# Batch 0's values loaded in packed rows and put in token order by selecting products, in an attention and mixer kernel

## The chip, the cores and the metric

One core of a Trainium2 chip runs the whole program. The metric is the device time of one execution in microseconds; three runs of the kernel before are given, with their median.

## The reference

Attention over 8 batches, 8 heads, 576 tokens of 64 values, with 16 extra ("beacon") keys and values ahead of each head's own, and after it a mixer: a low-rank product over the tokens and a two-layer product over the channels.

```python
k_all = np.concatenate([beacon_k, k], axis=2)
v_all = np.concatenate([beacon_v, v], axis=2)
scores = scale * np.matmul(q, k_all.transpose(0, 1, 3, 2))
scores = np.where(causal, -1000000000.0, scores)
a = np.exp(scores - scores.max(-1, keepdims=True))
a /= a.sum(-1, keepdims=True) + 1e-09
attn = np.matmul(a, v_all)                       # 8 x 8 x 576 x 64

x = attn.transpose(0, 2, 1, 3).reshape(8, 576, 512)
h = x.transpose(0, 2, 1) @ U @ V                 # U 576 x 32, V 32 x 576
u = x + h.transpose(0, 2, 1)
out = u + np.maximum(u @ w_ch1, 0.0) @ w_ch2     # 512 -> 2048 -> 512
```

Inputs and outputs are float32. The kernel works in float16 with float32 sums.

## The kernel before, in words

The attention goes by pairs of heads: 8 batches of 4 pairs are pairs 0 to 31, so pairs 0 to 3 are batch 0 and pairs 4 to 7 batch 1. The mixer's channel products go by 9 blocks of 512 tokens. Five engines work side by side: PE (matmul), DVE and ACT (elementwise, ACT alone does exponentials), POOL (here mainly the queue that issues casting loads) and SP (the queue of transposing transfers and of stores, and of batch 0's Q and K). Each engine runs its instructions in order. The order is written out by hand in a string, `SCRIPT`, of 961 steps; each step emits its instructions on the engines at that place. The names of the steps:

- `G`, `H`, `T`: for one pair, `Gq`/`Gk` regroups the main rows of Q or K into token order (and for batch 0 casts the head rows too, unless an `H` step does that), `H` casts the head rows, `T` turns them with five PE transposes into `tps` and copies the result to `qT` or `kT`. The letter behind says which engine copies (V DVE, A ACT, G POOL), the number which pair: `TkA7` is K of pair 7, copied by ACT.
- `Sa` to `Sd`: the scores of a pair in four groups of 496, 464, 496 and 208 columns for each of its two heads, on 64 partitions each (`sps`, L316), and ACT's exponentials into `expt` (L321). `Sa0:3` puts three filler matmuls ahead. There are four `expt` tiles, so a pair waits for the products of the pair two before it.
- `M`: DVE masks the exponentials of one head (L304, L306). `A`: PE's 15 products of the exponentials with V (`po`, L331), and DVE's division into `xb` (L339, L340).
- `I1`: one filler matmul of 512 columns into `idle` (L241).
- `X`: the low-rank part of one batch (`qtp`, `ups`, into `uT`). `g`, `U`, `p`, `P`, `F`: a block's first product (`gps`, L529, four matmuls a step, evacuated by ACT as `gT`, and DVE), transposes, sums and second products.
- `k`, `q`, `v`, `b`, `w`: loads on POOL's queue of K, Q, V, the beacon keys and weights (`w12` is quarter 2 of the first weights, which `g` steps 8 to 11 read), whole (all heads) or as half `A` or `B`. `u`, `s`, `c`, `e`: the loads and casts of the mixer's small matrices. `B` fills the mask.

Batch 0 loads Q and K through SP and ACT's queue into `stm` and `sth` in float32, pair by pair. Its V is loaded by `v0A` and `v0B`, the beacon rows and five tiles of tokens for each half of the heads:

```python
beacon_load(nc.gpsimd, bsrc, dst[:, 0, :, :], hs)
for j in range(NT):
    a = Nb if j == 0 else 0
    nc.gpsimd.dma_start(
        out=dst[a : a + nq[j], j, :, :], in_=src[hs, ds(q0[j], nq[j]), :].rearrange("h p d -> p h d")
    )
```

`nq` is 112, 128, 128, 128, 80. A partition of `vs` holds one token of each head (64 values, and a column of ones) for each of the five tiles. All PSUM tiles come from one pool of 8 banks. The pool `stage` (`st0`, `st1`) has two buffers for each name, and `loads` (`hd0`, `hd1`) too; a load into a new one waits until the old one's readers are through.

Of the kernel before, what the change touches and what calls it, by code (L numbers as in the profile page):

```python
# [27 lines left out]
def kernel(  # L28
# [82 lines left out]
    ident = const.tile([P, P], F16, name="ident", tag="ident")  # L111
# [80 lines left out]
    def beacon_load(eng, src, dst, hs):  # L192
        eng.dma_start(out=dst[0:Nb], in_=src[hs].rearrange("h p d -> p h d"))
# [4 lines left out]
    def v_loads(src, bsrc, vs, hs):  # L198
        dst = vs[:, :].rearrange("p (c h e) -> p c h e", h=H, e=E)[:, :, hs, 0:D]
# [589 lines left out]
    def step(t):  # L789
        name, arg = t[0], t[1:]  # L790
        if t == "guard":
            guard()
        elif t == "sum":
            guard_sum()
        elif name == "I":
            keep_warm(pst([P, 512], F32, name="idle"), int(arg))
        elif name in "kqbv":
            b, hs = int(arg[0]), HALVES[arg[1:]]
            if name == "k":
                k_loads(b, L_of(b), hs)  # L800
# [54 lines left out]
        Sd0 Sb0 Sa0:3 I1 GqV1 TqV1 GkV2 Sc0 I1 GqV2 v0B I1 I1 Sc1 Sb1 I1 M0.0 Sd1 M0.1 TqV2 TkV2 I1 A0.0  # L855
        I1 GqV3 Sa1:2 A0.1 M1.0 Sd2 I1 GkV3 q1A M1.1 Sc2 TqA3 Sb2 I1 k1A Sa2:1 TkV3 I1 M2.0 I1 A1.0 I1
        A1.1 Sd3 Sa3:1 w12 I1 Sb3 cV M2.1 GqV4 A2.1 b1 k1B TqV4 GkA5 Sc3 I1 GkV4 I1 M3.0 q1B eA GqV5
        TkV4 I1 GkV7 TkA5 I1 w13 A2.0 Sd4 M3.1 I1 TqV5 A3.0 GkA6 b2 w10 I1 A3.1 k2 Sa4 I1 Sd5 GqV6 GqV7
        TkA7 X0.0 X0.1 Sa5:0 X0.2 Sb4 TqV7 TqV6 Sc5 TkA6 v1A g0.9 Sc4 M4.1 Sb5 M5.1 U0.0 U0.2 g0.13
        GkV11 g0.1 M5.0 g0.10 g0.0 GkV8 g0.14 q2 g0.3 g0.11 GkA9 A5.0 A5.1 Sb7 I1 w11 TkV8 GqV8 GqV9 Sa7  # L860
        g0.2 M4.0 GqV11 Sd7 Sc7 TkV11 TkA9 g0.8 A4.1 M7.0 TqA9 A4.0 p00.0 p00.1 Sb6 v1B Sa6:0 g0.12
        p00.2 TqV11 M7.1 Sc6 g0.4 Sd6 g0.15 M6.0 GkA10 w20 U0.1 M6.1 TqV8 g0.6 A7.1 A7.0 Sd9 Sc9 w21
        A6.1 g0.7 A6.0 Sd8 g0.5 Sc8 Sa8 GqV10 X1.0 v2 b3 p01.0 p01.2 X1.1 P02.0 p01.1 X1.2 W0 P01.0 Sb8
        W4 W5 W1 Sb9 Sa9 W2 U1.1 W6 P01.1 TkA10 P02.1 M8.1 M9.0 TqA10 W7 b4 M8.0 U0.3 P05.0 P05.1 q3
        P06.0 P06.1 M9.1 A8.1 A9.0 A8.0 Sa10 P03.0 P03.1 k3 g1.15 A9.1 q4 Sa11 Sd10 g1.5 g1.1 Sb10 Sc10
        g1.3 g1.2 GkV13 GqA12 M10.0 GkA12 W3 P07.0 M10.1 P07.1 GqA13 Sb11 Sd11 GqA14 Sc11 M11.1 g1.9
        M11.0 GkA14 g1.12 A10.0 g1.7 g1.10 g1.0 R12 R13 R14 g1.6 TkV12 TqV12 TkV13 P04.0 GqA16 A11.1
        g1.8 U1.0 U1.3 TqA13 GkA15 P04.1 g1.14 A11.0 k4 A10.1 Sa13 Sd12 g1.11 p10.0 g1.4 GqA17 g1.13
# [160 lines left out]
```

## Time and profile before

| | |
|---|---|
| median of 3 runs | 339.31 us (338.8 to 339.33) |
| the profiled execution | 340.2 us, its span 338.5 us |
| granted clock of PE over the span | 0.999 |
| PE busy | 328.5 us, 3527 matmuls |
| DVE, ACT, POOL busy | 264.9, 227.9, 99.8 us |
| 384 matmuls L529 (`gps`) | 91.8 us, mean 379 ns |
| 256 exponentials L321 | 111.6 us, mean 538 ns |
| HBM read, written | 37.63 MB, 9.44 MB |

A row of a timeline gives the start in us from the span's start, the length, the engine, line and operation, what it writes and reads, how many instructions are merged (x), and in brackets how long the engine stood before it and what ended that. The length of merged rows runs from the first start to the last end, and neighbouring instructions of an engine overlap in their ends, so what an engine gives to one instruction is the distance between starts. A row of the loads gives their size as written and the median time from issue to landing.

### The profile page before, as it was taken

The numbers are of one execution on the slowest core, as the hardware profiler recorded it, in microseconds if no ns is written. First come the engines' busy times: TensorE is split into PE (matmuls) and PEld (weight loads), VectorE is DVE, ScalarE is ACT, GpSimd is POOL, SyncE is SP. The second block draws the span as 40 slices with busy tenths as digits, with TensorE's granted clock in tenths as the row PEclk, the third lists the DMA queues.
The fourth block names the chain that finished last, engine by engine and source line by source line (L and its number), as shares of the span: only waits on it lengthen the run. The fifth ranks groups of instructions, "written<-read, shape, count | busy, mean of one in ns | idle before, by whom it ended". The sixth has DMA issues, their size and how long they took to land.

```text
span 338.5 us, 8950 instructions
## 1 busy us (share of the span) xinstructions
PE 328.5 (97%) x3527; PEld 228.3 (67%) x3527; DVE 264.9 (78%) x690; ACT 227.9 (67%) x494; POOL 99.8 (29%) x129
## 2 busy tenths in 40 slices
PE   7889999999999999999999999999999999999994
PEld 3446465775678645765577547765688888888883
DVE  3788588985678857875888868886999999886872
ACT  4898898749688889878785799267912842644500
POOL 9756654350611602450025310000001503303300
PEclk9999999999999999999999999999999999999999
DMA  9999999999999999999979999454435501203033
GB/s 177 221 195 194 126 155 198 134 162 171 168 191 170 167 190 147 114 154 189 171 117 132 179 151 134 68 128 100 48 64 159 95 2 63 80 0 95 5 79 129
DMA packets 135600, 44.17 MB, mean 130 GB/s; under 512 B 108384, under 2 KB 130912, under 8 KB 135552
## 3 DMA queue, kind: packets, MB, share of 16 engines
q0 software_dynamic: 69008, 17.54, 61.4%
q1 hardware_dynamic: 65952, 25.66, 43.4%
q8 instruction: 29, 0.48, 0.6%
q10 hardware_dynamic: 592, 0.34, 0.3%
q14 instruction: 19, 0.16, 0.2%
HBM read 37.63 MB, written 9.44 MB: 139 GB/s over the span
## 4 chain that ended last, share of the span: by engine, by line
PE 69%; DVE 17%; DMA 6%; issue 3%; ACT 2%; SPq 1%; DVEq 0%; ACTq 0%
PE gps L529 21%; PE cpY L620 14%; PE cpD L620 7%; PE po L331 7%; PE sps L316 7%; DMA stm<-in_q_dram 4%; PE cpA L620 3%; PE fpY L566 3%; DVE gT L581 3%; DMA raw<-pr 3%; DVE ob L645 2%; DVE sT L601 2%; DVE uT L404 2%; PE fpD L566 2%; DVE xb L340 1%
## 5 line engine op out<-in xcount | busy, mean ns | idle before, releaser
L321 ACT ACTIVATE expt<-sps 128x496 f16<-128x496 f32 (+2 forms) x256 | 111.6, 538 | 16.1 <-PE sps L316 14.7
L529 PE MATMUL gps<-uT,w 128*128 128x512 f16 x384 | 91.8, 379 | 0.3 <-DVE ob L645 0.3
L620 PEld LDWEIGHTS <-gT 128*128 128x128 f16 x576 | 54.6, 98 | 10.5 <-issue 2.2
L529 PEld LDWEIGHTS <-w 128*128 128x128 f16 x384 | 34.4, 98 | 37.5 <-issue 2.5
L587 POOL TENSOR_SCALAR gT<-gT 128x512 f16<-128x512 f16 x12 | 17.8, 1495 | 105.6 <-DVE gT L581 89.0
L620 PEld LDWEIGHTS <-sT 128*128 128x128 f16 x432 | 40.9, 98 | 7.9 <-issue 2.0
L203 POOL DMA_DIRECT2D vs<-in_v_dram x50 | 40.6, 824 | 4.9 <-DMA w<-in_moe_w_ch_dram 2.5
L331 PEld LDWEIGHTS <-expt 128*128 128x128 f16 (+1 forms) x960 | 35.5, 98 | 9.5 <-DVE expt L304 1.5
L539 ACT ACTIVATE gT<-gps 128x512 f16<-128x512 f32 x48 | 29.7, 628 | 15.7 <-PE gps L529 15.2
L304 DVE TENSOR_TENSOR expt<-expt,bigmask 128x512 f16<-128x512 f16 x64 | 26.7, 418 | 17.1 <-ACT expt L321 17.1
L331 PE MATMUL po<-vs,expt 128*128 128x65 f16 (+1 forms) x960 | 38.1, 194 | 1.2 <-DVE expt L304 1.2
L620 PE MATMUL cpY<-wsum,gT 128*128 128x256 f16 x288 | 36.1, 273 | 0.0
L620 PE MATMUL cpD<-w,sT 128*128 128x256 f16 x288 | 35.5, 273 | 0.3 <-DVE sT L601 0.3
L316 PE MATMUL sps<-qT,kT 64*128 64x80 f16 (+4 forms) x384 | 34.6, 282 | 0.5 <-ACT kT L109 0.5
L340 DVE TENSOR_TENSOR xb<-po,rec 128x320 f16<-128x320 f32 x64 | 31.5, 492 | 2.2
L534 DVE SCALAR_TENSOR_TENSOR gT<-gps,gT 128x256 f16<-128x256 f32 x48 | 19.8, 420 | 15.1 <-ACT gT L533 14.9
L109 ACT ACTIVATE hP<-fpY 128x512 f32<-128x512 f32 x24 | 13.7, 598 | 23.0 <-PE fpY L566 18.8
L533 ACT ACTIVATE gT<-gps 128x256 f16<-128x256 f32 x48 | 19.4, 415 | 11.5 <-PE gps L529 11.0
L316 PEld LDWEIGHTS <-kT 64*128 64x128 f16 x384 | 14.0, 94 | 18.9 <-issue 10.1
L645 DVE TENSOR_TENSOR ob<-cpY,ut 128x512 f32<-128x512 f32 (+1 forms) x28 | 18.7, 667 | 6.0 <-PE cpY L620 6.0
L566 PEld LDWEIGHTS <-wf 128*128 128x128 f16 x192 | 18.6, 98 | 2.9 <-issue 0.7
L620 PE MATMUL cpY<-w,gT 128*128 128x256 f16 x144 | 17.7, 273 | 0.0
(115 smaller groups left out, 479.0 us busy)
## 6 DMA issues: line engine op xcount, KB each, us to landing
out_dram<-ob SPq DMA_DIRECT2D x16, 512.0 KB, 4.4
st<-in_k_dram POOLq DMA_DIRECT2D x6, 512.0 KB, 8.4
st<-in_q_dram POOLq DMA_DIRECT2D x6, 512.0 KB, 7.9
vs<-in_v_dram POOLq DMA_DIRECT2D x18, 128.0 KB, 7.8
w<-in_moe_w_ch_dram POOLq DMA_DIRECT2D x4, 512.0 KB, 8.8
w<-in_moe_w_ch_dram POOLq DMA_DIRECT2D x2, 1024.0 KB, 12.3
stm<-in_k_dram SPq DMA_DIRECT2D x4, 256.0 KB, 5.3
out_dram<-ob SPq DMA_DIRECT2D x4, 256.0 KB, 2.8
```

Source lines behind the costliest of these rows:

```text
L203: nc.gpsimd.dma_start(out=dst[a : a + nq[j], j, :, :], in_=src[hs, ds(q0[j], nq[j]), :].rearrange("h p d -> p h d"))
L304: nc.vector.tensor_tensor(out=e4, in0=e4, in1=bigmask, op=ALU.min)
L316: nc.tensor.matmul(ps[i][:, ds(o, w)], kT[hp, c, ds(P * ch, P)], qT[hp, c, ds(qa, w)], start=True, stop=True,)
L321: nc.scalar.activation(out=ex[i][:, ds(PAD + SLOT * g, gw[g])], in_=ps[i][:, 0 : gw[g]], func=AF.Exp, scale=scale)
L331: nc.tensor.matmul(po[:, j, :], ex[0 : nk[c], ds(blk[(c, j)], P)], vs[0 : nk[c], ds(c * H * E + h * E, E)], start=(c == 0), stop=(c == j),)
L340: nc.vector.tensor_tensor(out=xb[:, h // 2, :, ds(D * (h % 2), D)], in0=po[:, :, 0:D], in1=r.broadcast_to([P, NT, D]), op=ALU.mult)
L529: nc.tensor.matmul(g, w1[:, cc, ts(dc, P)], uT[:, cc, ds(ring(t0), 512)], start=(cc == 0), stop=(cc == NCC - 1))
L534: nc.vector.scalar_tensor_tensor(out=gT[:, dc, H2:512], in0=g[:, H2:512], scalar=0.0, in1=gT[:, dc, 0:H2], op0=ALU.max, op1=ALU.subtract,)
L539: nc.scalar.activation(out=gT[:, dc, :], in_=g, func=AF.Relu)
L566: nc.tensor.matmul(ps[:, i, :], a[:, kk, ts(2 * mp + i, P)], b[:, kk, :], start=opens and i == 0 and kk == 0, stop=kk == 1, skip_group_che ...
L620: nc.tensor.matmul(ps[:, i, :], a[:, f, ds(P * i, P)], b[:, f, :], start=opens and i == 0 and f == 0, stop=f == NK - 1, skip_group_check=True,
L645: nc.vector.tensor_tensor(out=out, in0=ps[:, ii, :], in1=other, op=ALU.add)
```

## The change

V of batch 0 is no longer loaded token by token. `packed_loads` (step `f0`) reads tokens 112 to 559 of all heads in rows of four tokens, one row of 1 KB per head and partition, into a staging tile `vf` on 112 partitions (it takes a buffer of `st0`). The first 112 tokens, the last 16 and the beacon rows are loaded in place, so there are four transfers in all. `unpack` (steps `DA1`, `DA2`, `DA3`, `DV4`) then makes one tile of `vs` each: four matmuls with a selecting matrix `pick` as weights, one for each token of a row, 512 columns on 32 partitions (16 for the last tile), add into one bank, and ACT (tiles 1 to 3) or DVE (tile 4) copies it to `vs`. `pick` is filled by DVE in step `B`.

```diff
+    VJ = 4
+    VG = P // VJ
+    VP = (S - nq[0]) // VJ // 16 * 16
+    VR = S - nq[0] - VP * VJ
+    pick = const.tile([P, VJ - 1 + P], F16, name="pick", tag="pick")
+
+    def fill_pick():
+        nc.vector.memset(pick, 0.0)
+        for g in range(VJ):
+            rows = ds(VG * g, VG)
+            nc.vector.tensor_copy(out=pick[rows, VJ - 1 : VJ - 1 + P : VJ], in_=ident[rows, rows])
...
+    def packed_loads(src, bsrc, vs, vf):
+        dst = vs[:, :].rearrange("p (c h e) -> p c h e", h=H, e=E)[:, 0, :, 0:D]
+        nc.gpsimd.dma_start(
+            out=vf[0:VP], in_=src[:, nq[0] : nq[0] + VP * VJ, :].rearrange("h (p j) d -> p h (j d)", j=VJ)
+        )
+        nc.gpsimd.dma_start(out=dst[Nb : Nb + nq[0]], in_=src[:, 0 : nq[0], :].rearrange("h p d -> p h d"))
+        last = vs[:, :].rearrange("p (c h e) -> p c h e", h=H, e=E)[:, NT - 1, :, 0:D]
+        nc.gpsimd.dma_start(
+            out=last[nq[NT - 1] - VR : nq[NT - 1]], in_=src[:, S - VR : S, :].rearrange("h p d -> p h d")
+        )
+        beacon_load(nc.gpsimd, bsrc, dst, ALLH)
+
+    def unpack(vf, vs, c, copy):
+        ps = pst([P, H, D], F32, name="vps")
+        n = min(P, VP * VJ - P * (c - 1))
+        rows = ds(VG * (c - 1), n // VJ)
+        for j in range(VJ):
+            nc.tensor.matmul(
+                ps[0:n], pick[rows, ds(VJ - 1 - j, n)], vf[rows, :, ds(D * j, D)], start=(j == 0), stop=(j == VJ - 1)
+            )
+        copy(out=vs[0:n, :].rearrange("p (c h e) -> p c h e", h=H, e=E)[:, c, :, 0:D], in_=ps[0:n])
...
+        elif name == "f":
+            late["f"] = stage.tile([P, H, 4 * D], F16, name="vf", tag="st0")
+            packed_loads(v[0], beacon_v[0], vss[0], late["f"])
+        elif name == "D":
+            unpack(late["f"], vss[0], int(arg[1:]), COPY[arg[0]])
...
         elif name == "B":
             fill_bigmask()
+            fill_pick()
...
-        HqA0 I1 GkA0 I1 I1 I1 GqA0 I1 I1 HkV0 u I1 I1 I1 GkV1 I1 B I1 I1 I1 TqA0 TkA0 I1 TkV1 I1 s v0A
+        I1 I1 I1 I1 I1 B GkA0 I1 I1 I1 I1 I1 GqV0 I1 I1 I1 I1 I1 HqA0 TqA0 I1 HkA0 TkA0 Sc0 I1 Sd0 Sb0
...
```

The first 295 steps of the script are replaced by 298: `v0A` and `v0B` by `f0` and four `D` steps, and the rest put in a new order, with the copying engine of 22 `G`, `H` and `T` steps exchanged. The 666 steps behind are the same, and so are the number of fillers and their size.

Three places show what moves. First ACT, from the last exponentials of pair 0 on. Before, those of pair 1 follow at once (`expt` 122 and 123 are pair 1's tiles):

```order
L321 ACTIVATE expt_120<-sps_294 128x496
L321 ACTIVATE expt_121<-sps_295 128x496
L321 ACTIVATE expt_122<-sps_318 128x496
L321 ACTIVATE expt_123<-sps_319 128x496
L321 ACTIVATE expt_122<-sps_328 128x464
L321 ACTIVATE expt_123<-sps_329 128x464
```
and now (tiles 123 and 124 are pair 1's):

```order
L355 ACTIVATE expt_121<-sps_267 128x496
L355 ACTIVATE expt_122<-sps_268 128x496
L109 ACTIVATE pr<-stm 128x512
L109 ACTIVATE hd_143<-sth 80x128
L109 ACTIVATE kT_125<-tps 128x80
L109 ACTIVATE kT_125<-tps 128x512
L109 ACTIVATE vs_127<-vps 128x8x64 x3
L109 ACTIVATE qT<-tps 128x64
L109 ACTIVATE qT<-tps 128x512
L109 ACTIVATE pr<-stm 128x512
L109 ACTIVATE hd_143<-sth 80x128
L355 ACTIVATE expt_123<-sps_384 128x464
```
The regrouping and turning of pair 1, which DVE copied before, the three unpacking copies and the regrouping of pair 2's Q now stand on ACT between the two pairs' exponentials.

Second ACT at the start of pair 0, where the head rows of K (`hd_142` now, cast by DVE before) come in between; before, and now:

```order
L109 ACTIVATE hd_142<-sth 80x128
L109 ACTIVATE pr<-stm 128x512 x2
L109 ACTIVATE qT<-tps 128x64
L109 ACTIVATE qT<-tps 128x512
L109 ACTIVATE kT_124<-tps 128x80
```
```order
L109 ACTIVATE pr<-stm 128x512
L109 ACTIVATE hd_143<-sth 80x128
L109 ACTIVATE qT<-tps 128x64
L109 ACTIVATE qT<-tps 128x512
L109 ACTIVATE hd_142<-sth 80x128
L109 ACTIVATE kT_125<-tps 128x80
```
The cast of K's head rows now stands behind the copies of qT, and the transposes of K need it.

Third POOL's queue of loads, up to the first weights (`w`). Before, behind the V loads of batch 0 and half of batch 1's Q and K:

```order
L203 DMA vs_126<-in_v_dram 80x4x64 [waits DMASW3_49]
L196 DMA st_429<-in_q_dram 128x4x256 [waits DMASW4_49]
L190 DMA hd_427<-in_q_dram 80x4x64 [waits DMASW5_49]
L196 DMA st_428<-in_k_dram 128x4x256 [waits DMASW6_49]
L190 DMA hd_426<-in_k_dram 64x4x64 [waits DMASW7_49]
L180 DMA w_108<-in_moe_w_ch_dram 128x4x512 [waits DMASW0_49]
```
and now:

```order
L202 DMA hd_277<-in_q_dram 80x4x64 [waits DMASW4_49]
L208 DMA st_537<-in_k_dram 128x8x256 [waits DMASW5_49,PE_49]
L202 DMA hd_535<-in_k_dram 64x8x64 [waits DMASW6_49,PE_49,Activation_49]
L205 DMA hd_535<-in_beacon_k_dram 16x8x64 [waits DMASW7_49]
L208 DMA st_538<-in_q_dram 128x8x256 [waits DMASW0_49]
L202 DMA hd_536<-in_q_dram 80x8x64 [waits DVE_49,DMASW1_49,PE_49,Activation_49]
L192 DMA w_108<-in_moe_w_ch_dram 128x4x512 [waits DMASW2_49]
```
All of batch 1's and batch 2's Q and K stand ahead of the first weights now, and batch 2's head rows wait for PE, DVE and ACT to be through with batch 0's, whose buffers they take.

More of the change, by code (lines that the diff above doesn't have):

```diff
@@ L853 @@
     SCRIPT = """
-        HqA0 I1 GkA0 I1 I1 I1 GqA0 I1 I1 HkV0 u I1 I1 I1 GkV1 I1 B I1 I1 I1 TqA0 TkA0 I1 TkV1 I1 s v0A
[L855 to L868, printed above, removed]
+        I1 I1 I1 I1 I1 B GkA0 I1 I1 I1 I1 I1 GqV0 I1 I1 I1 I1 I1 HqA0 TqA0 I1 HkA0 TkA0 Sc0 I1 Sd0 Sb0
@@ new lines @@
+        GkV1 I1 Sa0:3 q1A I1 GqA1 I1 f0 k1A GqV4 I1 TqV4 TkA1 I1 M0.1 M0.0 I1 GkV2 u s I1 DA2 DA1 DA3 I1
+        TqA1 TkV2 DV4 GqA2 Sb1 GkV3 Sd1 b1 Sc1 TqV2 I1 A0.0 Sa1:2 I1 A0.1 I1 GkV5 TkA3 Sb2 I1 k1B I1
+        GqV3 q1B M1.1 TkV5 GqV5 Sd2 TqA3 Sa2:1 I1 M1.0 GqV6 I1 k2 GkV4 b2 Sc2 cV q2 A1.1 I1 A1.0 Sb3
+        Sa3:1 w12 M2.1 w11 TqV6 Sd3 v1A TkV4 M2.0 I1 Sc3 A2.1 GkV6 TqA5 eA M3.1 I1 M3.0 A2.0 Sb4 A3.1
+        Sa4 I1 A3.0 Sc5 TkV6 w10 Sd4 GkV9 X0.0 Sd5 X0.2 X0.1 Sc4 TkA9 GqV8 GkV7 Sb5 GqV7 Sa5:0 GkV8 g0.9
@@ new lines @@
+        TkV8 g0.10 TqV7 M5.1 M5.0 TkV7 GqA9 g0.11 g0.5 M4.1 TqA8 g0.4 TqV9 A5.0 b4 g0.0 v1B A5.1 w13 Sc7
+        g0.7 GqV11 GqV10 Sd7 Sa7 M4.0 Sb7 M7.1 g0.6 g0.1 A4.0 A4.1 M7.0 Sa6:0 Sb6 g0.3 g0.2 Sd6 w20 w21
+        GkV11 Sc6 M6.0 A7.1 A7.0 g0.8 g0.13 GkV10 Sc9 p00.0 Sb9 U0.1 M6.1 Sa9 g0.14 p00.2 TkV11 TqA10
+        A6.1 g0.15 A6.0 g0.12 p00.1 X1.0 Sd9 p01.0 TqV11 X1.1 v2 p01.1 U0.0 P01.0 X1.2 W4 W5 W0 W1 Sd8
+        TkA10 W2 P01.1 Sa8 Sc8 W6 q3 p01.2 U0.2 Sb8 P02.0 P02.1 U0.3 P05.0 P05.1 P06.0 P06.1 M8.1 P03.0
@@ L869 @@
+        GqV12 W7 P03.1 M9.1 g1.3 M8.0 k3 A8.1 g1.2 g1.5 A9.1 GqA13 M9.0 GkV13 g1.1 A8.0 b3 Sd10 Sa10
+        GkA12 g1.14 A9.0 g1.9 GqV14 g1.7 Sb10 Sa11 Sd11 P07.0 P07.1 W3 Sc11 Sb11 R12 R13 GkV14 Sc10
+        M11.0 M11.1 g1.0 g1.8 M10.1 M10.0 g1.15 TkV12 g1.6 U1.1 R14 U1.3 TqV12 U1.0 q4 g1.12 TkV13 P04.0
+        g1.10 P04.1 GkV15 TqA13 A10.0 A11.1 A11.0 GqA16 k4 A10.1 Sa13 Sd12 g1.11 p10.0 g1.4 GqA17 g1.13
         Sa12 Sb12 Sc12 p11.0 GqV15 X2.0 M12.0 P11.0 GkA17 P11.1 U1.2 X2.1 GkV16 p11.1 R15 P12.0 P12.1
```

## The prediction

> **What bounds the kernel now.** I read the page first (busy shares, then the chain that ended last), then the busy times by stretch, and then the timelines of TensorE (PE) and ScalarE (ACT) over the first 40 us, where the change lies.
>
> ```profile
> span 338.5 us, 8950 instructions
> PE 328.5 (97%) x3527; PEld 228.3 (67%) x3527; DVE 264.9 (78%) x690; ACT 227.9 (67%) x494; POOL 99.8 (29%) x129
> PE 69%; DVE 17%; DMA 6%; issue 3%; ACT 2%; SPq 1%; DVEq 0%; ACTq 0%
> ```
> PE is busy for 97% of the span and carries 69% of the chain. The stretches before and after the first block step `g` differ, though:
>
> ```profile
> 6.90:36.30 29.40, 27.00 (x358) 15.55 (x357) 24.22 (x87) 25.21 (x64) 18.93 (x28) 1.00 1.57 197
> 36.30:90.50 54.20, 54.20 (x595) 34.45 (x594) 41.32 (x115) 42.15 (x102) 23.65 (x32) 1.00 1.64 161
> ```
> The columns are PE, PEld, DVE, ACT, POOL busy. From 36.3 us on PE never stands: whatever is done by then sets the end, and time lost later on another engine costs nothing. Before that, PE has holes and `idle` fillers, and ACT is busy for 25.2 of 29.4 us. Two rows frame this start, and the next shows where both kernels issue the same rest:
>
> ```profile
> 1.59 5.50 PE L241 MATMUL idle<-ident 128*128 128x512 f16 x13 [1.59 <-POOL ident masks.py:199]
> 6.92 0.20 PE L261 MATMUL tps<-ident,hd 80*128 80x80 f16 x1
> 34.57 1.02 PE L529 MATMUL gps<-uT,w 128*128 128x512 f16 x4
> 90.54 1.08 PE L331 MATMUL po<-vs,expt 128*128 128x65 f16 x30
> ```
> First transpose at 6.92, first `g` step (g0.9) at 34.57; PE's order from the row at 90.54 on is the same in both kernels. So the result is: how much later or earlier does PE reach its first `g`, and how much work has it then behind it. The change removes 12 V transfers, but does PE wait for V?
>
> ```profile
> 8.78 0.46 PE L316 MATMUL sps<-qT,kT 64*128 64x208 f16 x4 [0.47 <-ACT kT L109]
> 13.59 0.21 PE L261 MATMUL tps<-ident,hd 80*128 80x80 f16 x1 [0.60 <-DVE hd L741]
> 14.35 0.62 PE L331 MATMUL po<-vs,expt 128*128 128x65 f16 x15
> 23.51 0.63 PE L331 MATMUL po<-vs,expt 128*128 128x65 f16 x15 [1.23 <-DVE expt L304]
> ```
> These are PE's three waits of the start (0.47 + 0.60 + 1.23 = 2.3 us) and its first product with V, at 14.35, which waits for nothing. None of the waits is for V: they end with ACT's and DVE's copies and masks. So the change pays only through what else it moves.
>
> **Part by part.** *The first pair's start.* Two more fillers stand ahead of the first transpose (15 for 13). A warm filler takes 0.22 us (14.80 to 15.02 below), so that transpose starts at 7.1 + 0.2, some 0.4 us later. Then a longer detour: HkA0 (the K head's cast) is ACT's work now, and stands behind ACT's copies of qT.
>
> ```profile
> 14.80 0.38 PE L241 MATMUL idle<-ident 128*128 128x512 f16 x1
> 15.02 0.59 PE L241 MATMUL sps<-ident 128*128 128x512 f16 x2
> 5.54 0.31 ACT L109 ACTIVATE hd<-sth 80x128 f16<-80x128 f32 x1 [1.62 <-DMA sth<-in_q_dram]
> 5.75 1.14 ACT L109 ACTIVATE pr<-stm 128x512 f16<-128x512 f32 x2
> 7.39 0.71 ACT L109 ACTIVATE qT<-tps 128x64 f16<-128x64 f16 x2 [0.50 <-PE tps L263]
> 7.99 0.73 ACT L109 ACTIVATE kT<-tps 128x80 f16<-128x80 f16 x2
> 9.07 5.71 ACT L321 ACTIVATE expt<-sps 128x208 f16<-128x208 f32 x14 [0.35 <-PE sps L316]
> ```
> Copies of qT now from 7.8 (7.39 + 0.4) to 8.4, where ACT takes the next instruction (7.39 to 7.99 is 0.6); the head's cast 0.31, to 8.7; K's transposes on PE 0.3 and the way to ACT 0.25, to 9.25; copies of kT 0.73, to 10.0; the scores and the way back 0.35 to 0.45. The first exponential starts at about 10.4 in place of 9.07: +1.3 us. In the old order DVE had cast that head and K's transposes ran during the copies of qT.
>
> *ACT up to the first g.* It takes 27.2 us from its first exponential to the first `g` (9.07 to 36.31), and waits in it 1.18 + 0.54 + 0.34 + 0.94 = 3.0 us:
>
> ```profile
> 15.97 2.53 ACT L321 ACTIVATE expt<-sps 128x496 f16<-128x496 f32 x6 [1.18 <-PE sps L316]
> 24.75 1.06 ACT L321 ACTIVATE expt<-sps 128x496 f16<-128x496 f32 x2 [0.54 <-PE sps L316]
> 26.76 0.72 ACT L109 ACTIVATE kT<-tps 128x80 f16<-128x80 f16 x2 [0.34 <-PE tps L263]
> 28.09 0.63 ACT L109 ACTIVATE pr<-st 128x512 f16<-128x512 f16 x1
> 29.66 1.53 ACT L321 ACTIVATE expt<-sps 128x496 f16<-128x496 f32 x4 [0.94 <-PE sps L316]
> 36.31 0.73 ACT L539 ACTIVATE gT<-gps 128x512 f16<-128x512 f32 x1
> ```
> So 24.2 us of work. What the new order adds ahead of g0.9: three copies of unpacked V, 128x512 from PSUM. No row has one; the nearest are the cast of `pr` from f32 (1.14 / 2 = 0.57) and a qT step (0.6 by starts, its last part 128x512 from PSUM). With 0.5 to 0.6, 1.5 us. GqA1 and GqA2, 2 x 0.57, with their heads 2 x 0.25 (0.31, and 0.2 by starts at 5.54 and 5.75): 1.6. Five steps of transposes copied by ACT (TkA1, TqA1, TkA3, TqA5, TkA9) for three gone (TkA5, TkA7, TkA6): 2 x 0.6 = 1.2. Gone too GkA5 and GkA6, 2 x 0.6 = -1.2 (28.09). Scores Sc4 and Sb5 now stand before g0.9, with exponentials of 2 x 496 and 2 x 464 columns, at 5.71 us for 5664 columns (the row at 9.07): 1.9. Together +5.0 us. DVE gives up several copies for this and gains one unpack copy; it is not late in this stretch. The memsets and copies of `pick` run on DVE before its first data, at 5 to 6 us, and cost nothing.
>
> Without any wait ACT reaches g0.9 at 10.4 + 24.2 + 5.0 = 39.6. I take that: ACT was the busiest after PE, and with 5 us more in front of it, it will hardly wait; with the same waits it would be 42.6. PE runs ahead of it. In the old run the lead is 36.31 - 34.57 = 1.7 us; in the new order Sc4, TkA9, Sb5 and Sa5 (1.0 + 0.6 + 0.9 + 1.0 of ACT's time) stand right ahead of g0.9, and their outputs and the `g` take 2 + 1 + 2 + 2 + 1 = 8 PSUM banks, all there are, so the lead can be 3.0. First g on PE: 39.6 - 3.0 = 36.6, which is **+2.0 us**.
>
> *PE.* Unpacking adds 16 matmuls of 512 columns on 16 or 32 partitions. Nearest rows: fillers of 512 columns at 0.22 us, and
>
> ```profile
> 31.49 0.28 PE L397 MATMUL ups<-Vsb,qts 32*128 32x240 f16 x4
> ```
> where four matmuls on four different row groups take 0.28 us together. Here four of one chunk share a row group and accumulate, so they go one after another; only neighbouring chunks can overlap. Bounds 16 x 0.22 = 3.5 and 13 x 0.22 = 2.9; I take 3.0. The Trainium skill (TensorE: Matmul & The Clock Gate, Why this matters for your kernels) says that a matmul with 32 contraction rows takes as long as one with 128, and that the gain lies in running row groups side by side. By it, chunks issued in turn would take a third, about 1 us (an estimate from that page's 3.07 times); this order issues them chunk by chunk, so the rule speaks against the change. The row at 31.49 agrees that row groups overlap; no row here shows four on one group. PE alone could pay this: 34.57 + 0.4 + 3.0 + 0.2 for the other moved steps, less its old waits (2.3 shown; 3.2 with the ends of the instructions ahead of them), is 35.0, before 36.6. So ACT, not PE, sets it.
>
> *Work already done at the first g.* All of the old order's PE work but TkA7 and TqV7 (2 x 0.27), and in addition Sc4 (0.3), Sb5 (0.2), a transpose for pair 9 (0.27) and a filler with its turn (0.3): 0.5 us more, 0.9 if fewer changes of matmul shape in the remainder are counted. I take **-0.7 us**.
>
> *Loads.* V comes in four transfers in place of 12, behind q of batch 1. K and Q of batch 2 now stand ahead of the first weights `w12` on POOL's queue, and their heads wait for TkA3 and TqA3 on PE: by ACT's sum 10.4 + 3.4 (pair 0, 3328 columns) + 1.4 (GqA1, TkA1) + 1.5 + 1.4 (TqA1, GqA2) + 3.4 (pair 1) = 21.5, and some 2 us after it. Behind those wait w12, w11, V of batch 1 and w10.
>
> ```profile
> 15.07 0.75 POOL L180 DMA_DIRECT2D w<-in_moe_w_ch_dram  x1 [0.47 <-DMA vs<-in_v_dram]
> w<-in_moe_w_ch_dram POOLq DMA_DIRECT2D x3, 512.0 KB, 8.2
> st<-in_q_dram POOLq DMA_DIRECT2D x1, 256.0 KB, 7.1
> ```
> w12 goes from 15.07 to about 25 and lands at 33 (issue to landing 8.2): 3 us ahead of g0.9 at 36.6. w10 waits on POOL's queue for w12's landing and lands 7 to 8 us behind it, at 40 to 41; g0.0, which reads it, comes five `g` steps of 0.9 and as many other steps after 36.6, at 42. Hidden, with 1 to 3 us of cover. V's packed rows are issued third, at 4 us; with 7 to 9 us to landing they are there at 11 to 13. PE comes to the first unpack at 13.8 at the soonest, since its bank comes free with pair 0's last exponential (10.4 + 3.4): hidden, with about 1 us.
>
> *Sum.* +2.0 - 0.7 = +1.3 us on the profiled execution, which took 340.2 us (span 338.5), so 341.5. The median of the runs shown is 339.31, 0.9 below that; the same step gives **340.6 us**. A difference of 0.2% (0.7 us) is about what a measurement of this kernel can tell from none.
>
> **Rivals.** *Loads were what held the start (faster).* Before 12 us,
>
> ```profile
> DMA packets 5861, 2.35 MB, mean 196 GB/s; under 512 B 4173, under 2 KB 5861, under 8 KB 5861
> 9.11 7.46 DMA stm<-in_q_dram
> ```
> 4173 of 5861 packets are under 512 B, most of them V's; the last Q of batch 0 is 7.46 us under way and stands in the chain. With 2688 packets fewer (448 tokens of 8 heads in rows of four) Q and K land earlier, ACT and DVE never starve, and PE runs without waits: first g at 35.0 (above), +0.4 - 0.7, and the remainder loses up to 0.7 less at PE's waits for banks: -1.0, 338.3 us. It decides if ACT's work fits in 38 us, 1.6 less than I sum. The Trainium skill (DMA: Bandwidth & Descriptors, Specifications) puts 512 B as the least size for line rate, which is this rule; the packet row shows the sizes, and no wait of PE shows the price. Against it: PE's waits end with ACT and DVE.
>
> *V lands late.* PE is in order: behind the first unpack stand pair 1's transposes and scores. If the 448 KB behind q of batch 1 take 12 us, PE stands from 13.8 to 16 and ACT with it: 340.6 + 2 = 342.6.
>
> *Weights late.* If POOL's waits for the heads come 3 us later, w12 or w10 pass their cover by some 2.5: 340.6 + 2.5 = 343.1.
>
> *No difference.* ACT ends 1 us sooner than summed, within 0.7 of 339.31.
>
> **How the numbers follow.** Forecast (slower, 340 to 341.8) 0.38; no difference 0.18; loads held the start 0.24; V late 0.10; weights late 0.10. Slower by over 0.2%: 0.38 + 0.10 + 0.10 = 0.58. The range reaches from the faster rival, less 0.1 for unpacking at 2.9 and 0.6 for hidden waits in front of more instructions, 337.6, to the late weights with 0.7 us of waits on ACT besides, 343.8; less than 0.2 lie outside.
>
> **What would show it.** First exponential at 10.4, not 9.07; ACT without gaps from 19 to 39 us; PE's first `gps` at 36.6; the row of 30 `po` matmuls, at 90.54 now, at about 91.8; unpack matmuls 0.22 apart. Wrong if the first `gps` starts before 35.5, if PE waits at `vps` for a DMA, or if a `g` step waits for `w`.

## The result

The changed kernel takes 341.79 us (median of 4 runs, 341.23 to 342.19), the kernel before 339.32 in the same set (4 runs): the ratio is 1.0075, 95% interval 1.0056 to 1.0093, so +2.5 us. A second set, run later, gave 341.26 (12 runs) against 339.62 (23 runs): 1.0046, interval 1.002 to 1.0071, +1.6 us. The forecast was 340.6 and slower; both medians lie in its range (337.6 to 343.8).

The page of the changed kernel (span, busy time by engine, then the chain that ended last):

```profile
span 339.9 us, 8984 instructions
PE 329.4 (97%) x3543; PEld 228.5 (67%) x3543; DVE 266.9 (79%) x697; ACT 227.3 (67%) x496; POOL 94.9 (28%) x121
PE 74%; DVE 18%; issue 3%; ACT 3%; POOL 0%; DVEq 0%; ACTq 0%; POOLq 0%
```
The 6% of DMA in the chain of before are gone from it, and PE has 16 matmuls more. The timeline of PE, the rows that answer to those of before:

```profile
1.59 5.84 PE L275 MATMUL idle<-ident 128*128 128x512 f16 x15 [1.59 <-POOL ident masks.py:199]
7.27 0.20 PE L295 MATMUL tps<-ident,hd 80*128 80x80 f16 x1
...
8.69 0.21 PE L295 MATMUL tps<-ident,hd 80*128 80x80 f16 x1 [0.78 <-ACT hd L109]
...
9.94 0.39 PE L350 MATMUL sps<-qT,kT 64*128 64x336 f16 x6 [0.82 <-ACT kT L109]
...
14.19 1.06 PE L236 MATMUL vps<-vf,pick 32*128 32x512 f16 x12
15.18 0.39 PE L275 MATMUL idle<-ident 128*128 128x512 f16 x1
...
16.02 1.05 PE L236 MATMUL vps<-vf,pick 16*64 16x512 f16 x4
17.49 0.68 PE L350 MATMUL sps<-qT,kT 64*128 64x464 f16 x10 [0.42 <-ACT qT L109]
...
30.62 0.64 PE L365 MATMUL po<-vs,expt 128*128 128x65 f16 x15 [0.20 <-DVE expt L338]
...
36.69 1.04 PE L563 MATMUL gps<-uT,w 128*128 128x512 f16 x4
...
90.49 2.00 PE L365 MATMUL po<-vs,expt 128*128 128x65 f16 x60
...
333.22 1.04 PE L654 MATMUL cpY<-wsum,gT 128*128 128x256 f16 x8
```
and of ACT:

```profile
10.36 3.38 ACT L355 ACTIVATE expt<-sps 128x496 f16<-128x496 f32 x8 [0.48 <-PE sps L350]
...
15.26 1.58 ACT L109 ACTIVATE vs<-vps 128x512 f16<-128x512 f32 x3 [0.23 <-PE vps L236]
16.70 0.73 ACT L109 ACTIVATE qT<-tps 128x64 f16<-128x64 f16 x2
...
39.43 1.19 ACT L573 ACTIVATE gT<-gps 128x512 f16<-128x512 f32 x2
```
PE's first `gps` is 2.12 us later than before (36.69 for 34.57). The way from the first transpose to it grew from 27.65 to 29.42 us, by 1.77: unpacking takes 0.99 (14.19 to 15.18) and 4 x 0.22, so 1.9, and the waits stay about as long as they were, 0.78 + 0.82 + 0.42 + 0.20 = 2.2 for 2.3. None of the old waits was for V, and the new order has others of the same length. By the row of 30 `po` matmuls, from which on both kernels issue the same, 1.25 of the 2.12 are given back, mostly because more work is done by then: eight score matmuls and a filler more, five transposes fewer. That row starts at 91.41 (it is the second half of the row of 60 from 90.49) for 90.54, and the last group of matmuls at 333.22 for 332.72.

Both kernels were profiled a second time (the runs are told below). From the second profile of before (PE):

```profile
6.54 0.20 PE L261 MATMUL tps<-ident,hd 80*128 80x80 f16 x1
...
33.87 1.02 PE L529 MATMUL gps<-uT,w 128*128 128x512 f16 x4
...
89.84 1.08 PE L331 MATMUL po<-vs,expt 128*128 128x65 f16 x30
...
331.52 1.04 PE L620 MATMUL cpY<-wsum,gT 128*128 128x256 f16 x8
```
and from that of the changed kernel:

```profile
6.38 0.20 PE L295 MATMUL tps<-ident,hd 80*128 80x80 f16 x1
...
13.80 1.06 PE L236 MATMUL vps<-vf,pick 32*128 32x512 f16 x12 [0.44 <-DMA vf<-in_v_dram]
...
36.32 1.04 PE L563 MATMUL gps<-uT,w 128*128 128x512 f16 x4
...
90.13 2.00 PE L365 MATMUL po<-vs,expt 128*128 128x65 f16 x60
...
332.87 1.04 PE L654 MATMUL cpY<-wsum,gT 128*128 128x256 f16 x8
```
Here the first `gps` is 2.45 us later, the row of 30 `po` matmuls 1.21 (91.05 for 89.84) and the last group of matmuls 1.35. In this run the start came early (first transpose at 6.38), and PE waited for the packed V. The executions of one kernel differ by up to 3 us (before, 338.73 to 341.62 in the 23 runs; changed, 340.75 to 343.87 in the 12). The spans close 5.8 us (both profiles of before) to 6.7 and 6.3 us (changed) behind the start of the last group; nothing in the change explains that (the kernel with fewer fillers, told below, has the change and closes 5.8 behind too). In the first profile of the changed kernel the last four stores are issued over 4.28 us, in the other four over 3.02; why the ends differ stays open.

The transfers issued in the first 12 us of the changed kernel, after the packets the issues with their sizes and median time to landing:

```profile
DMA packets 3946, 2.24 MB, mean 187 GB/s; under 512 B 1354, under 2 KB 3946, under 8 KB 3946
stm<-in_k_dram SPq DMA_DIRECT2D x4, 256.0 KB, 6.4
stm<-in_q_dram SPq DMA_DIRECT2D x3, 256.0 KB, 7.3
vf<-in_v_dram POOLq DMA_DIRECT2D x1, 448.0 KB, 10.6
sth<-in_k_dram SPq DMA_DIRECT2D x4, 32.0 KB, 6.7
```
and the same transfers of K and Q in the kernel before:

```profile
stm<-in_k_dram SPq DMA_DIRECT2D x4, 256.0 KB, 5.3
stm<-in_q_dram SPq DMA_DIRECT2D x3, 256.0 KB, 6.1
sth<-in_k_dram SPq DMA_DIRECT2D x4, 32.0 KB, 5.1
```
Packets under 512 B fell from 4173 to 1354, as the change says, but no more bytes came (2.24 MB for 2.35) and K and Q of batch 0 take 1.1 to 1.6 us longer to land.

### The profile page after: what moved, and what is told of

Same layout as the page of the kernel before. It is cut to its first block, busy times and chain, and to the rows that moved or that the text cites. A ratio compares the mean times of both kernels' runs of the same rounds, so it can differ in the third digit from the quotient of the medians.

```text
span 339.9 us, 8984 instructions
## 1 busy us (share of the span) xinstructions
PE 329.4 (97%) x3543; PEld 228.5 (67%) x3543; DVE 266.9 (79%) x697; ACT 227.3 (67%) x496; POOL 94.9 (28%) x121
## 4 chain that ended last, share of the span: by engine, by line
PE 74%; DVE 18%; issue 3%; ACT 3%; POOL 0%; DVEq 0%; ACTq 0%; POOLq 0%
PE gps L563 22%; PE cpY L654 15%; PE cpD L654 7%; PE sps L350 7%; PE po L365 7%; PE cpA L654 3%; PE fpY L600 3%; DVE gT L615 3%; PE idle L275 3%; DVE ob L679 2%; DVE sT L635 2%; DVE uT L438 2%; PE fpD L600 2%; DVE xb L374 1%; PE tps L297 1%
## 5 line engine op out<-in xcount | busy, mean ns | idle before, releaser
L654 PEld LDWEIGHTS <-gT 128*128 128x128 f16 x576 | 54.7, 98 | 10.3 <-issue 2.0
L573 ACT ACTIVATE gT<-gps 128x512 f16<-128x512 f32 x48 | 29.0, 623 | 15.4 <-PE gps L563 14.9
L350 PE MATMUL sps<-qT,kT 64*128 64x80 f16 (+4 forms) x384 | 33.8, 282 | 1.4 <-ACT kT L109 0.8
L215 POOL DMA_DIRECT2D vs<-in_v_dram x40 | 33.4, 853 | 2.3 <-DMA st<-in_q_dram 2.1
L109 ACT ACTIVATE hP<-fpY 128x512 f32<-128x512 f32 x24 | 13.7, 598 | 23.0 <-PE fpY L600 22.0
```

Of the source, the lines that this page charges most:

```text
L215: nc.gpsimd.dma_start(out=dst[a : a + nq[j], j, :, :], in_=src[hs, ds(q0[j], nq[j]), :].rearrange("h p d -> p h d"))
L350: nc.tensor.matmul(ps[i][:, ds(o, w)], kT[hp, c, ds(P * ch, P)], qT[hp, c, ds(qa, w)], start=True, stop=True,)
L573: nc.scalar.activation(out=gT[:, dc, :], in_=g, func=AF.Relu)
L654: nc.tensor.matmul(ps[:, i, :], a[:, f, ds(P * i, P)], b[:, f, :], start=opens and i == 0 and f == 0, stop=f == NK - 1, skip_group_check=True,
```

## The experiments

All are timed against the kernel before, run beside them on the same chip. The edits are in `SCRIPT` unless said otherwise.

**ScalarE's unpack copies to VectorE.**

```diff
- DA2 DA1 DA3
+ DV2 DV1 DV3
```


> The changed kernel with the three unpack copies of ScalarE (1.58 us of its time, 15.26 on) given to VectorE, which waits there. Theory 'ScalarE sets the start' (the prediction's): ScalarE reaches the first g step 1.5 us sooner, the first gps goes from 36.69 to about 35.2, the kernel from 341.8 to about 340.4. Theory 'TensorE's own instructions set it' (of its 29.4 us from the first transpose to the first gps only 2.2 are shown as waits): the first gps stays at 36.5 to 36.9, the kernel within 0.5 us of the changed one.

Measured: 341.53 us, 1.0041 of before (1.0022 to 1.006). PE's timeline:

```profile
1.59 4.87 PE L275 MATMUL idle<-ident 128*128 128x512 f16 x15 [1.59 <-POOL ident masks.py:199]
6.30 0.20 PE L295 MATMUL tps<-ident,hd 80*128 80x80 f16 x1
...
15.04 1.06 PE L236 MATMUL vps<-vf,pick 32*128 32x512 f16 x12 [1.76 <-DMA vf<-in_v_dram]
...
37.40 1.04 PE L563 MATMUL gps<-uT,w 128*128 128x512 f16 x4
```
and ACT's first copy behind the unpacking:

```profile
16.73 0.71 ACT L109 ACTIVATE qT<-tps 128x64 f16<-128x64 f16 x2 [2.68 <-PE tps L297]
```
From the first unpack matmul to the first `gps` it is 22.36 us, in the changed kernel 22.50 and 22.52. Of the 1.5 us taken off ACT only some 0.8 count: ACT stands 2.68 us until the transposes behind the unpacking are done, and takes the copy shown 1.69 us behind the first unpack matmul, in the changed kernel 2.51 (16.70 less 14.19). Of these 0.8 us 0.14 arrive at the first `gps`, so ACT does not set that stretch. Neither theory had the new row: PE waits 1.76 us for the packed load, although up to there the instructions are those of the changed kernel. In this run V took 11.5 us to land, for 10.6 and 10.3.

**No fillers from the first scores to the first `g` step.**

```diff
- Sc0 I1 Sd0 ... GkV8 g0.9
+ Sc0 Sd0 ... GkV8 g0.9        (20 I1 gone)
```
The fillers inside the `Sa` steps stay.

> The changed kernel without the 20 idle matmuls between the first scores and the first g step (20 x 0.22 = 4.4 us of TensorE; those ahead of the first transpose stay). Theory 'ScalarE sets the start': the waits of TensorE grow by what the fillers took, the first gps stays at 36.7 within 0.3, the kernel at 341.8 or, if the granted clock falls in the holes, above it. Theory 'TensorE's own instructions set it': the first gps comes 3 to 4 us sooner, until ScalarE's work bounds it, and the kernel goes to 338 to 339.

Measured: 341.59 us, 1.0055 (1.0037 to 1.0072). It settles nothing on its question: PE waited 2.9 us for V, up to 15.15, and ran at a granted clock of 0.78, 0.50 and 0.58 in the three stretches from 15 to 24 us; the first `gps` came at 38.75.

**The K head's cast on VectorE, as before.**

```diff
- HkA0 TkA0
+ HkV0 TkA0
```


> The changed kernel with the cast of pair 0's K head on VectorE, as before (HkV0 for HkA0). Both theories put the first exponential at about 9.4 in place of 10.36, since K's transposes no longer wait for ScalarE (TensorE's wait of 0.78 us goes). ScalarE: 0.31 us less work and a start 0.9 sooner, first gps 35.7 to 35.9, kernel 340.9. TensorE: only the 0.78 and what is left of the 0.82 wait go, first gps 35.7 to 36.0, kernel 341.0. If the loads set the next steps (the packed V lands at about 14.1), the gain is lost there: TensorE waits at vps for a DMA and the first gps stays at 36.5.

Measured: 341.48 us, 1.0057 (1.0023 to 1.009). From the first transpose to the first exponential it is 2.27 us for 3.09, so the detour over ACT cost 0.8, close to the 0.9 expected; but in the profiled execution the gain goes into the next wait. PE at the unpacking, and then PE's and the other engines' busy times by stretch (behind them the granted clock, the DMA share and GB/s):

```profile
14.66 1.68 PE L236 MATMUL vps<-vf,pick 32*128 32x512 f16 x12 [2.12 <-DMA vf<-in_v_dram]
```
```profile
12.00:15.00 3.00, 0.88 (x9) 0.29 (x10) 2.13 (x12) 1.30 (x5) 0.10 (x1) 1.00 1.42 237
15.00:18.00 3.00, 3.00 (x24) 1.45 (x17) 0.10 (x1) 1.69 (x5) 0.59 (x2) 0.50 1.46 219
18.00:21.00 3.00, 3.00 (x18) 1.22 (x17) 1.96 (x4) 1.95 (x6) 2.19 (x3) 0.50 1.62 197
```
PE waits 2.1 us for V and is then granted half the clock until 24 us. In this execution the first `gps` came at 40.80. It is the longest of the 12 (345.67 us): four took 344.04 to 345.67, the other eight 340.61 to 341.51, and the median of these eight, about 340.95, is near the 340.9 and 341.0 that the two theories gave. So the gain may well arrive when V is there in time; the one profile can't show it.

**The new order alone**, with V loaded as before and no unpacking.

```diff
- f0 ... DA2 DA1 DA3 ... DV4
+ v0A v0B
```


> The changed order of instructions, but V of batch 0 loaded as before, by 12 transfers into token order, at the place of the packed load, and no unpacking. ScalarE theory: 1.5 us of copies gone, first gps 35.2, kernel 340.3. TensorE theory: 12 + 4 matmuls (about 1.0 + 0.9 us) and the 0.42 wait behind them gone, first gps 34.6 to 34.9, kernel 339.7 to 340. Rival 'the loads held the start': small packets delay Q and K of the next pairs, the gain is lost, 341.5 or more, with DMA waits in TensorE's or VectorE's rows before 36 us.

Measured: 342.14 us, 1.0081 (1.0049 to 1.0112). With 1.9 us of PE work and 1.5 of ACT gone, the kernel is no faster than the changed one: the third theory of the expectation held, a gain lost to a transfer. The 12 V transfers stand on POOL's queue ahead of K of batch 1, which is issued at 15.81 us for 6.15 in the changed kernel, and PE waits for that:

```profile
21.47 0.21 PE L295 MATMUL tps<-ident,hd 80*128 80x80 f16 x1 [1.67 <-DMA hd<-in_beacon_k_dram]
```
The granted clock is 0.61 and 0.82 in the two stretches from 21 to 27 us, and the first `gps` comes at 37.44. So in the new order the packing is worth about what its unpacking costs. Both halves of V stand together here; with the second half further back, as before, the new order was not run.

**The packing alone**, in the old order, the packed load first on POOL's queue.

```diff
- s v0A ... v0B ... A0.0
+ s f0 ... DV1 DV2 DV3 DV4 A0.0
```


> The order of before with the packing alone: one packed load (f0) where the first V transfers were issued and none of the later ones, and the four unpack steps (matmuls, copies on VectorE) put ahead of the first product with V. The first kernel cell of a two by two with the changed order with old loads (342.14 against 340.01 before, ratio 1.008). Theory 'the new order is what costs, the packing alone is worth its price': between 338.5 and 340, no wait for vf on TensorE, first gps at 34.6 to 36 (unpacking 1.9 us of TensorE, part of it in the old waits of 2.3 us). Theory 'the start is bounded by V's landing in any order': TensorE waits at vps for a DMA here too and the kernel is slower than before by 1 us or more. Theory 'small V packets delayed Q and K': first gps before 34.0 and kernel under 339.

Measured: 346.84 us, 1.0196 (1.0157 to 1.0234). Neither of the two theories of a gain holds, and the second had the wrong transfer: PE waits for the first K, not for V. The granted clock is 0.54 from 12 to 15 us and 0.60 from 21 to 24. DVE's row, then PE's:

```profile
10.60 0.22 DVE L775 CAST hd<-sth 80x128 f16<-80x128 f32 x1 [2.65 <-DMA sth<-in_k_dram]
```
```profile
10.88 0.21 PE L295 MATMUL tps<-ident,hd 80*128 80x80 f16 x1 [3.33 <-DVE hd L775]
```

**The packed load first, in the new order.**

```diff
- q1A I1 GqA1 I1 f0 k1A GqV4 I1 TqV4 TkA1 ... DV4 GqA2
+ f0 q1A I1 GqA1 I1 k1A I1 TkA1 ... DV4 GqV4 TqV4 GqA2
```


> The changed kernel with the packed load first on GpSimd's queue, ahead of q of batch 1, and the steps that need that q (GqV4 TqV4) behind the unpack steps. Theory 'V lands too late' (in three runs TensorE waited 1.8 to 2.9 us at vps until 14.7 to 15.2): vf is issued at 1.9 in place of 3.5 and lands 1.5 us sooner, the wait at vps goes below 0.5 us, the first gps comes at 35 to 36 and the kernel at 340.3 to 340.9. Theory 'ScalarE sets the start': first gps stays within 0.4 of 36.7 to 37.4 and the kernel at 341.5 to 341.8. If the wait only moves to q of batch 1: a wait at the transposes of GqV4, and no gain.

Measured: 343.71 us, 1.0124 (1.0071 to 1.0177). V is there when PE comes to it, at 13.38, and the wait turns up at q of batch 1, with a clock of 0.68 and 0.75 from 18 to 24 us behind it:

```profile
17.73 0.21 PE L295 MATMUL tps<-ident,hd 80*128 80x80 f16 x1 [1.46 <-DMA hd<-in_q_dram]
```

**Unpacking later**, behind pair 1's transposes and scores.

```diff
- DA2 DA1 DA3 I1 TqA1 TkV2 DV4 GqA2 Sb1 GkV3 Sd1 b1 Sc1
+ I1 TqA1 TkV2 GqA2 Sb1 GkV3 Sd1 DA2 DA1 DA3 b1 Sc1 DV4
```


> The changed kernel with three unpack steps moved behind pair 1's transposes and its first two scores, and the fourth behind all its scores (work that needs no V). Theory 'V lands too late': TensorE fills the time to the landing with pair 1, no wait at vps, first gps 35.5 to 36.3, kernel 340.5 to 341. If the copies of the unpacked V on ScalarE, now behind two exponentials, hold the first product with V: TensorE waits at the first po for 0.5 to 1.5 us and the gain is lost. ScalarE theory: no change, 341.8.

Measured: 341.69 us, 1.0048 (1.0026 to 1.0071), as the changed kernel beside it. There is no wait at `vps` (16.80), one of 0.67 for pair 1's K head instead, and the first `gps` comes at 37.59, 29.86 behind the first transpose (changed kernel 29.42 and 29.94). Moving the unpacking out of the way of the landing gains nothing.

**The changed kernel again.**

> The changed kernel unchanged, beside the other three and its own set of runs of before. From the three kernels that waited for V: its profile shows either the first transpose at 6.3 and a wait at vps of 1 to 2 us, or the first transpose at 7.2 and none; in both the first gps lies at 36.7 to 37.5. The time: ratio 1.0075 within 0.002, 341.5 to 342.5.

Measured: 341.26 us, 1.0046 (1.002 to 1.0071); the rows are above. The first `gps` at 36.32 is 0.4 sooner than the earliest that was expected, since the wait for V was only 0.44, and the time and the ratio lie below their expected ranges too (341.5 to 342.5, 1.0055 to 1.0095).

**Fewer fillers**: the 12 between the unpacking and the first `g` step gone, those before it kept.

```diff
- DA3 I1 TqA1 ... TqV2 I1 A0.0 ... GkV8 g0.9
+ DA3 TqA1 ... TqV2 A0.0 ... GkV8 g0.9        (12 I1 gone)
```


> The changed kernel without the 12 idle matmuls between the unpacking and the first g step; those before it stay, so that TensorE does not stand before V lands. Measured from the first unpack matmul to the first gps, which was 22.5 us in two runs of the changed kernel, and 22.4 with 1.5 us of copies taken off ScalarE. Theory 'TensorE's own instructions set it': 12 x 0.22 to 0.26 = 2.6 to 3.1 us fewer, less short new waits (1.2 us in the run without any filler): 20.3 to 21.5, kernel 340 to 340.8. Theory 'ScalarE sets it, the fillers only fill': 22.3 to 22.6, as many us of waits more, kernel 341.3 to 341.8. In both the granted clock must stay at 1.00, or the run tells nothing on this.

Measured: 340.51 us, 1.0025 (1.0007 to 1.0043); the clock stayed at 1.00. PE, then the first gap over 0.2 us that ACT shows after 15.06:

```profile
13.99 1.06 PE L236 MATMUL vps<-vf,pick 32*128 32x512 f16 x12
...
21.35 0.40 PE L297 MATMUL tps<-ident,pr 128*128 128x128 f16 x4 [0.46 <-DVE pr L287]
...
29.44 0.64 PE L365 MATMUL po<-vs,expt 128*128 128x65 f16 x15 [0.34 <-DVE expt L338]
...
35.74 1.04 PE L563 MATMUL gps<-uT,w 128*128 128x512 f16 x4
```
```profile
42.91 0.38 ACT L567 ACTIVATE gT<-gps 128x256 f16<-128x256 f32 x1 [1.07 <-PE gps L563]
```
The stretch is 21.75 us, 0.75 shorter, for 2.6 to 3.1 us of fillers. It lies between the two theories: PE's own instructions held the first `gps` by 0.75 us, and behind them the other engines follow so closely that the rest returns as waits (PE's listed ones of 0.1 us and more are 1.6 us from the unpacking on, for 0.6). ACT's missing gaps alone don't show that it limits now: the changed kernel's ACT has none over 0.2 us either, from 15.26 to 43.85. But there five exponentials take 0.20 to 0.32 us longer from start to start than others of their size, 1.25 us together; here one does, by 0.62 us. No run took work off both engines. This is the best kernel with the change, 0.7 us ahead of it by the medians of the second set and of this one, and still behind the kernel before.

**The packed load first, q of batch 1 used later.**

```diff
- DV4 GqV4 TqV4 GqA2 ... Sc1 TqV2 I1 A0.0        (against the kernel with the packed load first)
+ DV4 GqA2 ... Sc1 TqV2 GqV4 TqV4 I1 A0.0
```


> The packed load first on GpSimd's queue as in the run that had it so (343.71, first unpack at 13.4, then 1.5 us of TensorE waiting for q of batch 1 and a lower clock after it), and the steps that need that q (GqV4 TqV4) moved behind pair 2's transposes, 3 us later. Theory 'the transfers of the first 18 us set the start, in the order in which they are queued': no wait at vps, none or under 0.5 us for q of batch 1, clock 1.00, first gps 35.5 to 36.5, kernel 340.5 to 341.2. If the transfers as a whole are too many for that time: a wait for another of them takes its place (k of pair 1 to 3 or q of batch 1), 341.5 or more.

Measured: 343.21 us, 1.0115 (1.0081 to 1.0149). The same transfer lands later still, and PE waits for it 1.54 us, at 19.02. With V in q's place in the queue it is q that comes too late, in both places where it was used.

**The kernel before again.**

> The kernel before, unchanged, profiled a second time. In its first profile the last matmul starts at 333.5 and the span ends 5.0 us behind it; nine profiles of kernels with the changed code or order end 5.2 to 5.9 behind. If that first profile was an execution with a late start of TensorE's full clock and a short end, as its 340.2 beside a median of 339.3 to 340.0 lets one think: first transpose at 5.8 to 6.4, last matmul at 332.3 to 333.0, so 0.6 to 1.7 us ahead of the changed kernel's 333.6 and 334.0. If not: 333.5 within 0.2, and the difference of the medians is not in TensorE's sequence.

Measured: 339.83 us in 12 runs (338.75 to 341.95, and one of 347.15), 1.0012 of the other runs of before (0.999 to 1.0034). The rows are above: the last group of matmuls at 331.52, 1.2 us ahead of the first profile. So that first profile was a late execution (340.2 us) and the second an early one (339.05); the +0.5 us at the end of PE that the first shows against the changed kernel is too small. The first transpose, 6.54, is a little later than the 5.8 to 6.4 expected. The end is as short in both (span 337.3), so the expectation on the end was wrong.

**The old order with the packed load behind q of batch 1**, as in the changed kernel, bigmask and `pick` built at the start, three copies on ACT.

```diff
- s v0A ... GqV2 v0B ... TkV2 I1 A0.0 I1 GqV3 Sa1:2 A0.1 ... GkV3 q1A
+ s q1A f0 ... GqV2 ... TkV2 I1 DA2 DA1 DA3 DV4 I1 GqV3 Sa1:2 A0.0 A0.1 ... GkV3
```


> The old order of steps with the packing alone once more (the first such kernel took 346.84: its packed load, first on GpSimd's queue, ran beside the first K, whose head landed 7.8 us after its issue, and TensorE stood 3.3 us and lost clock). Now the packed load stands as in the changed kernel, behind q of batch 1, bigmask and pick are built at the start, and the four unpack steps stand ahead of the first product with V, three copies on ScalarE. Theory 'the transfers' order did it, the packing's own price is the unpacking': no wait over 1 us before the first exponential (8.9 to 9.5), first gps 34.5 to 36, kernel 340 to 341.5. Theory 'one large transfer beside the first K and Q costs wherever it stands early': the first exponential at 10 or later, or a wait at vps over 1 us, kernel 342 or more. Theory 'the new order of steps is what costs, not the packing': under 340.

Measured: 344.97 us, 1.0146 (1.0123 to 1.0169). PE:

```profile
9.21 0.21 PE L295 MATMUL tps<-ident,hd 80*128 80x80 f16 x1 [1.64 <-DVE hd L775]
...
16.05 0.21 PE L295 MATMUL tps<-ident,hd 80*128 80x80 f16 x1 [2.04 <-DVE hd L775]
...
39.27 1.02 PE L563 MATMUL gps<-uT,w 128*128 128x512 f16 x4
```
The clock stays at 1.00 here, so this is the price in waits alone: PE's listed waits up to the first `gps` are 0.52 + 1.64 + 2.04 + 1.09 + 0.35 = 5.6 us for 2.3 before. The two large ones end with casts of K and Q of batch 0 that DVE makes late because the transfers land late. In both places tried near the front, the old order stands the packed V beside the first K and Q badly. Here q of batch 1 came forward with it, so the two are not parted.

## Why the prediction was right, and where it was not

**The start** was right. Two more fillers ahead of it: the first transpose lies at 6.32 in the mean of four runs with 13 fillers (5.84 to 6.92) and at 6.78 in the mean of ten with 15 (6.30 to 7.73), +0.46 for the 0.4 given; with rows that lie over 1 us apart it is partly luck that this is so close. The detour of HkA0: 3.09 us from the first transpose to the first exponential for 2.15 (2.31 in the second profile of before), and 0.8 of it gone when the cast went back to DVE.

**"So ACT, not PE, sets it"** is the step that failed, although its number, a first `gps` at 36.6, was met (36.69, 36.32). ACT's own sum was good: its first exponential at 10.36 for 10.4, its copy of the first `gps` at 39.43 for 39.6, and no listed gap over 0.15 us from 19 to 39 us, as said. That an engine shows no gaps does not make it the one that limits. With 0.8 us off ACT the stretch from the first unpack matmul shrank by 0.14; with fillers off PE it shrank by 0.75. The error was in the sum that was set aside, PE alone: 35.0 let all old waits go and none come. With the waits left in (2.2 for 2.3), unpacking at its true 1.9 and the other moved steps as given, that sum is 34.57 + 0.35 + 1.9 + 0.2 - 0.1 = 36.9, within 0.25 of what came. So two sums met in one place, and that the one taken gave the right number is luck. ACT is some 0.75 us behind.

**Unpacking** was mis-sized: 3.0 us, measured 1.9. The 12 matmuls of three chunks stand in the program chunk by chunk, and yet ran three at a time, each chunk on its own row group: 0.99 us in place of 2.6. The fourth chunk took 4 x 0.22. In the changed kernel other instructions stand between it and the three; but in the run with the packing alone it stands right behind them and starts behind them all the same (19.02 for 17.94), so why it does not join them stays open. The Trainium skill (TensorE: Matmul & The Clock Gate, Why this matters for your kernels) puts the gain in running row groups side by side, and the trace agrees: three groups took 0.99 us for 12 matmuls, 2.7 times faster than one after another. The 1 us estimated from that page was for all 16, which took 1.9. That this order misses the gain was the prediction's own addition, and wrong.

**Work already done** was sized too low: 0.7, measured 1.25 and 1.24 in the two pairs of profiles (2.12 less 0.87, 2.45 less 1.21).

**Loads.** Weights: hidden, as said; no `g` step waits for `w`. V: "hidden, with about 1 us" was wrong. It lands at 13.7 to 15.1 us, not 11 to 13, because it takes 10.2 to 11.6 us for the 7 to 9 assumed (seven profiles with V in this place of the queue). In the changed kernel PE came to it just in time once and waited 0.44 us once, which the prediction had named as a sign of being wrong; in the run with the unpack copies on VectorE, the same up to there, it waited 1.76, and in two variants that came sooner 2.1 and 2.9. The rival "V lands late" thus held its mechanism, at 0 to 1.8 us in the kernel as changed, and it can swallow a faster start.

**The rival "loads were what held the start"** had its cause the wrong way round. Small packets did go, and K and Q of batch 0 landed later. All of V and half of q and k of batch 1 are now queued by 7.5 us, while 12 V transfers at 0.7 us of issue each had spread themselves to 10.8 us. The rate did not rise: the stretch from 0 to 18 us before, and then in the changed kernel,

```profile
0.00:18.00 18.00, 15.35 (x128) 7.20 (x129) 10.35 (x54) 11.92 (x29) 14.54 (x29) 1.00 1.31 199
```
```profile
0.00:18.00 18.00, 14.40 (x96) 6.34 (x96) 8.22 (x47) 11.46 (x28) 9.40 (x22) 1.00 1.16 201
```
shows 199 and 201 GB/s (last column). The Trainium skill (DMA: Bandwidth & Descriptors, Specifications) has 512 B as the least size for line rate; here a third of the small packets gave no more bytes in the same time. In the old order the kernel with the packed load is 5 to 7 us behind before, in the new one about 2; the new order is largely what makes the packing bearable. What delays K and Q is in part the order of the queue: in the new order with the 12 small transfers the three rows shown above take 5.7, 6.9 and 6.1 us, between those of before (5.3, 6.1, 5.1) and of the changed kernel (6.4, 7.3, 6.7). That the rest is the size of the early transfer is read from these landing times and from the two kernels in the old order; no run paced the packed load by itself.

**The sum**: +1.3 forecast; at the row of 30 `po` matmuls +0.87 and +1.21 (a start later than said, more work done than said), on PE's last group +0.5 and +1.35 in the two pairs of profiles, +2.5 and +1.6 in the medians. The medians thus show about 1 us more than PE's end does in the mean. The longer end behind the last matmul (6.7 and 6.3 us for 5.8) would be most of that; executions that wait for V would add to it (the run with the unpack copies on VectorE, which waited 1.76 us, has its last group at 334.04), but so few profiles can't say how many do. Neither was settled.

## What to carry to other kernels

Before costing a cheaper transfer, look whether the bottleneck engine waits for it at all; in the kernel before it never did, and the packing brought 1.9 us of matmuls with no wait to take away. In the new order it did take one away: there the 12 transfers kept K of batch 1 back. One large transfer early is not 12 small ones made cheaper: here it was queued at once, and what the first steps need landed 1.1 to 1.6 us later. Where engines run within a microsecond of each other, test which one limits by taking work off each; an engine without gaps and a sum that meets the number may still name the wrong one.

## What the runs showed of the hardware

A wait of PE can cost more than its length. In eight runs PE stood 1.4 us or more between 9 and 22 us, for a transfer or for a cast that waited for one. In six of them the granted clock was between 0.50 and 0.86 in the stretches of 3 us behind it, one to four of them (the 2.12 us wait shown above: 0.50 until 24 us), and in two it was not (waits of 1.76, and of 1.64 and 2.04). The figures between are means: the traces' own records of the clock hold 1.00 and 0.50 alone, and in the start 0.50 lasts 3.41, 6.83 or 10.24 us, so one, two or three times 3.41. A long wait is not needed for it: in the run with the packing alone half the clock came a second time, from 21.6 to 25.0 us, behind listed waits of 0.32 and 0.29. The Trainium skill (TensorE: Matmul & The Clock Gate, Part 1: The HAM clock gate) has a gate that watches a free-running window of some 3.4 us, by which such a difference would hang on where the wait falls in the window. The lengths agree with that window; a wait of 1.46 us was enough once, and how much of the window PE must stand was not measured.

The fillers ahead of the first transpose show the same lottery: they start 0.43 us apart up to a point between 4.5 and 7.5 us, and 0.22 us apart behind it (6.5 in the first profile of the changed kernel, 4.6 in the run with the unpack copies on VectorE). So the same 15 took 5.84 us in the one and 4.87 in the other, and the first transpose moved with them by 1 us.
